# Order edges on VectorE, spread loads and two more half buffers in a Strassen matmul chain on one Trainium2 core

## The chip, the cores and the metric

One core of a Trainium2 chip runs the whole program. TensorE (PE) multiplies, ScalarE (ACT) and VectorE (DVE) work on elements, SyncE (SP) issues every DMA of the part that changes, GpSimd (POOL) has almost nothing to do. Each engine takes its instructions in the order written for it and waits at an instruction whose inputs or whose output buffer are not ready. The metric is the device time of the program in microseconds (us), lower is better.

## The reference

```python
# q, k, v: 8 x 8 heads x 576 x 64
q_s = np.exp(q - np.max(q, axis=-1, keepdims=True))
q_s = q_s / (np.sum(q_s, axis=-1, keepdims=True) + 1e-09)
...                                            # k_s the same, along axis 2
kv = np.einsum('bhsd,bhse->bhde', k_s, v)
attn_out = np.einsum('bhsd,bhde->bhse', q_s, kv)
x = np.ascontiguousarray(attn_out.transpose(0, 2, 1, 3)).reshape(B * S, H * D)   # 4608 x 512
...
h = x @ w_in                                   # first pair of weights, 512 -> 2048 -> 512
g = h * (1.0 / (1.0 + np.exp(-1.702 * h)))
x = g @ w_out
...
h = x @ w_in                                   # second pair of weights, the same sizes
g = np.where(h >= 1, h, np.where(h <= -1, 0.0, (h + 1) ** 2 / 4))
out = g @ w_out
```

The weights arrive in float64 and are converted on the chip.

## The kernel before

The scheduler of the language decides the order on each engine: the program is written in one order, and rows of an engine may be moved past each other by the scheduler's own estimate of when inputs are there. An order edge (`add_manual_dep` with `NoSync`) fixes that one row stands behind another on the same engine; it adds no semaphore.

**Stages.** (1) Attention and the first matrix `x @ w1_in` run block by block: 9 blocks (`NB`) of 512 tokens, 16 steps (`NM`) each (`gemm1`, `act`, lines 720 to 742); results `g0` go to DRAM, one store per two steps from one of three buffers `sg`. (2) `out_pass(0, ...)` computes `g @ w1_out`. (3) `pass_in` computes `x1 @ w2_in` and the activation, stores `g1`, and in its first part also converts `w2_out` ("the last weight's conversion"). (4) `out_pass(1, ...)` computes `g1 @ w2_out`.

**Strassen form.** Stages 2 to 4 multiply 2 x 2 block matrices with seven products instead of eight, in the order `PROD = (1, 7, 6, 2, 5, 4, 3)`. A matrix product in float32 is done as three matmuls, with each operand split into a high and a low part: `hi` is a rounded copy (ACT, line 104), `lo = src - hi` (DVE, line 105). The operands of products 7, 6 and 5 are sums of two quadrants and need a DVE instruction before the split (`operand`, through `tt`, line 108, "SUM" below); products 1, 2, 4 and 3 take a quadrant as it stands. Product 2 is followed by `last_sum`, which makes the operand of product 4.

**An out pass.** 5 column groups `j` (`HALVES`: 512, 512, 512, 384, 384 columns), 7 products, 4 pieces `i` of the inner dimension: 140 steps, 28 per group. In a group, steps 0 to 3 are product 1, 4 to 7 product 7, 8 to 11 product 6, 12 to 15 product 2, 16 to 19 product 5, then 4 and 3. A step is 12 matmuls (`gemm`), and behind `gemm(s)` stands `ready(s + 3)`, which makes the operand pair three steps ahead. The pairs live in 7 slots (`R_AT` = 16, 17, 18, 19, 24, 25, 26) taken in turn: `hi` of step s takes the slot that `lo` of step s - 4 had, `lo` of step s that of `hi` of step s - 3. So `hi(s)` can start once gemm(s - 4) is through, and `lo(s)` once gemm(s - 3) is.

**Slots.** 27 tiles of 128 x 1024 float32, named `s0` to `s26`: 0 to 15 hold the four quadrants (`G_AT`), in `pass_in` 4 to 15 and 20, 21 its operand pairs (`C_AT`), 22 to 26 its results on their way to DRAM (`E_AT`), 16 to 19 the weight conversion (`W_AT`: raw data, halves, sums, and `hls`, the output buffers of 256 elements x 2). Seven weight buffers `w` of 2 MB serve all passes in turn.

**Between the passes.** The first steps of an out pass are prepared in the last steps of the stage ahead (`ready0`, `ready1`), and its quadrants and weights are loaded there. Slots 24 to 26 are not free yet at that time: ahead of pass 0 slots 20 to 26 do not exist until the first stage's buffers are released, ahead of pass 1 slots 22 to 26 hold results that are being stored. A DMA that SP issues waits for the DMA issued eight before it.

Of the kernel before, what the change touches and what calls it, by code (L numbers as in the profile page):

```python
# [8 lines left out]
FP32 = mybir.dt.float32  # L9
FP32R = mybir.dt.float32r  # L10
# [3 lines left out]
ALU = mybir.AluOpType  # L14
# [4 lines left out]
def kernel(  # L19
# [11 lines left out]
    nc = tc.nc  # L31
# [8 lines left out]
    NM = DFF // P  # L40
# [61 lines left out]

    def split(hi, lo, src):
        nc.scalar.activation(out=hi, in_=src, func=ACTF.Copy)  # L104
        nc.vector.tensor_tensor(out=lo, in0=src, in1=hi.bitcast(FP32), op=ALU.subtract)  # L105

    def tt(o, x, y, op):
        nc.vector.tensor_tensor(out=o, in0=x, in1=y, op=op)  # L108


    def weight_sets(width, raws, f12, f_r, f_s, hls):
# [70 lines left out]
    def load_weight(sl, w, p):  # L182
        sl[p] = wslot()
        nc.sync.dma_start(out=sl[p].bitcast(FP32), in_=wp_dram[w, p])
# [5 lines left out]

    def operand(bq, p, i):
        b11, b12, b21, b22 = (bq[qd][i] if qd in bq else None for qd in ("11", "12", "21", "22"))
        if p == 7:
            tt(b12, b22, b12, ALU.subtract)
        elif p == 6:
            tt(b11, b12, b11, ALU.add)
        elif p == 5:
            tt(b12, b22, b11, ALU.subtract)
        return {1: b11, 7: b12, 6: b11, 2: b21, 5: b12, 4: b21, 3: b22}[p]


    def last_sum(bq, i):
# [25 lines left out]
    def slot(i, dt=FP32):  # L228
        return rooms["s", i].tile([P, 2, TB], dt, tag=f"s{i}", name=f"s{i}")
# [35 lines left out]
    class Tokens:  # L265
# [9 lines left out]

        def ready(self, j, p):
            n = HALVES[j]
            src = operand(self.t[j], p, 0)
            hi, lo = (slot(C_AT[p] + i, FP32R)[:, :, :n] for i in range(2))
            split(hi, lo, src)  # L280
            self.ops[j, p] = hi, lo
            if p == 2:
                last_sum(self.t[j], 0)


    def out_pass(ph, gq, sl):
        ops = {}
        zs = {}

        steps = [(j, p, i) for j in range(NJ) for p in PROD for i in range(4)]  # L290

        def ready(s):
            if s >= len(steps):
                return
            j, p, i = steps[s]
            src = operand(gq.t[j], p, i)
            n = HALVES[j]
            hi, lo = (slot(R_AT[(2 * s + x) % len(R_AT)], FP32R)[:, :, :n] for x in range(2))
            split(hi, lo, src)
            ops[s] = hi, lo  # L300
            if p == 2:
                last_sum(gq.t[j], i)

        def gemm(s):
            j, p, i = steps[s]
            n = HALVES[j]
            if p in OPENS and i == 0:
                zs[Z_OF[p]] = bank(OPENS.index(p))
            z = zs[Z_OF[p]]
            hi, lo = ops.pop(s)  # L310
            w = sl[p]
            for m in range(2):
                for c in range(2):
                    o = slice(c * 256 + m * P, c * 256 + (m + 1) * P)
                    wh, wl = w[:, 0, i, o], w[:, 1, i, o]
                    trio = ((wh, hi), (wh, lo), (wl, hi))
                    for x, (a, b) in enumerate(trio):
                        nc.tensor.matmul(  # L318
                            out=z[:, m, :n], lhsT=a, rhs=b[:, c, :],
                            start=(p in OPENS and i == 0 and c == 0 and x == 0),  # L320
                            stop=(i == 3 and c == 1 and x == 2),
                            skip_group_check=True,
                        )

        late = []

        def store(j, a, b, t):
            n, t0 = HALVES[j], STARTS[j]
            if not ph:
                nc.sync.dma_start(out=x1_dram[j, a, b], in_=t)  # L330
            else:
                late.append((j, a, b, t))

        def turn():
            for j, a, b, t in late:
                n, t0 = HALVES[j], STARTS[j]
                n4 = n // 4
                pt = bank(2, "pt").rearrange("p a c -> p (a c)").rearrange("p (r d) -> p r d", r=4)
                for r in range(4):
                    for m in range(2):  # L340
                        nc.tensor.transpose(  # L341
                            out=pt[:n4, r, m * P:(m + 1) * P], in_=t[:, m, r * n4:(r + 1) * n4], identity=ident
                        )
                u = slot(23).rearrange("p a c -> p (a c)").rearrange("p (r d) -> p r d", r=4)
                nc.scalar.activation(out=u[:n4], in_=pt[:n4], func=ACTF.Copy)
                r0 = t0 + b * n
                nc.sync.dma_start(
                    out=out[r0:r0 + n, a * 256:(a + 1) * 256].rearrange("(r p) d -> p r d", r=4),
                    in_=u[:n4],
                )  # L350
            late.clear()

        tmp = {}

        def post(j, p):
            n = HALVES[j]
            z = zs[Z_OF[p]][:, :, :n]

            def new(name):
                at = O_AT[name] if name in O_AT else (20 if ph else 23)  # L360
                return slot(at)[:, :, :n]

            def keep(name):
                t = new(name)
                nc.scalar.activation(out=t, in_=z, func=ACTF.Copy)
                return t

            if p == 1:
                zs["x"] = bank(3, "zx")
                nc.scalar.activation(out=zs["x"][:, :, :n], in_=z, func=ACTF.Copy)  # L370
            elif p == 7:
                tmp["s7"] = keep("s7")
            elif p == 6:
                tmp["u2"] = keep("u2")
            elif p == 2:
                store(j, 0, 0, keep("c11"))
            elif p == 5:
                tt(tmp["s7"], tmp["s7"], z, ALU.add)
                store(j, 1, 1, tmp["s7"])
            elif p == 4:  # L380
                tt(tmp["u2"], tmp["u2"], z, ALU.add)
                store(j, 1, 0, tmp["u2"])
            else:
                store(j, 0, 1, keep("c12"))

        LA = 3

        def run(hooks, done):
            for s in range(done, LA):
                ready(s)  # L390
            for s, (j, p, i) in enumerate(steps):
                gemm(s)
                if i == 2 and ph:
                    turn()
                if i == 3:
                    post(j, p)
                    if j + 1 < NJ:
                        for qd in {2: ("11",), 5: ("12",), 4: ("22", "21")}.get(p, ()):
                            gq.load(j + 1, qd)
                    else:  # L400
                        for f, a in hooks.get(p, ()):
                            f(*a)
                ready(s + LA)
            if ph:
                turn()

        return ready, run


    def pass_in(xq, sl, hooks):  # L410
        wr = [slot(i).rearrange("p a c -> p (a c)") for i in W_AT]
        load_set, convert_set, sum_set = weight_sets(
            128, [wr[0]], [wr[1][:, :512], wr[1][:, 512:]], wr[2][:, :512], wr[2][:, 512:768],
            [wr[3][:, :512], wr[3][:, 512:]],
        )
        n_new = [0]
        zs = {}
# [93 lines left out]
    with ExitStack() as st0:  # L511
# [234 lines left out]
        def at(s, f, *a):  # L746
            todo.append((s, len(todo), f, a))
# [39 lines left out]
                at(s0 + 4 + part + 0.5, sum_set, w, si, part)  # L787
        for p in PROD[:3]:
            at(NM + 8 * 12 + 1, load_weight, w_out1, "out1", p)
        for i, p in enumerate(PROD[3:]):  # L790
            at((NB - 1) * NM + 4 * i + 3, load_weight, w_out1, "out1", p)
        for i in range(2):
            at(NB * NM - 3 + i, ready0, i)
        todo.sort(key=lambda t: t[:2])
        jobs = {}
        for key, _, f, a in todo:
# [38 lines left out]
        for s in range(NB * NM):  # L835
            if s == (NB - 1) * NM:
                st1.close()
                open_room("s0", "left", range(NH), [P, 2, TB])
                open_room("p1", "left", (2, 3), [P, 2, TB])
                for qd in ("11", "12", "22", "21"):  # L840
                    g0.load(0, qd)
            gemm1(s)
            if s % 2 == 1:
                act(s)
            for f, a in jobs.get(s, ()):
                f(*a)
        widen(3, w_out1[1])
        widen(2, w_out1[1])
    open_room("s1", "right", range(NH, 27), [P, 2, TB])

    hooks = {p: [(load_weight, (w_in2, "in2", p))] for p in PROD}
    hooks[2].insert(0, (xq.load, (0,)))
# [5 lines left out]
    def lw(p):  # L858
        return load_weight, (w_out2, "out2", p)
# [3 lines left out]
        7: [lw(7), (g1.load, (0, "12", (2, 3)))],  # L863
        6: [(g1.load, (0, "22", (0, 1))), (ready1, (0,))],
        2: [(g1.load, (0, "22", (2, 3))), lw(6), (ready1, (1,))],
        5: [(g1.load, (0, "21", (0, 1)))],
        4: [(g1.load, (0, "21", (2, 3))), lw(2)],
        3: [lw(5), lw(4), lw(3)],
    }
    pass_in(xq, w_in2, hooks)  # L870
    run1({}, 2)


# [28 lines left out]
```

## Time and profile before

| what | value |
|---|---|
| median of 3 runs | 1627.42 us (1627.15 to 1629.46) |
| the profiled execution | 1628.26 us, span from first to last instruction 1626.5 us |
| PE busy | 1573.0 us (97%) |
| DVE, ACT busy | 1154.4 us (71%), 946.9 us (58%) |
| mean granted TensorE clock | 0.992 |
| DMA over the span | 202 GB/s |

PE is the engine to look at: what it doesn't work, and where it works at a lower clock, is what a change of order can win. A busy share near 100% in a stage says that nothing else decides there.

### The profile page before, as it was taken

What the parts mean: (1) busy time and instruction counts of PE and PEld (TensorE: products, weight loads), DVE (VectorE), ACT (ScalarE), POOL (GpSimd) and SP (SyncE); (2) the same over time, 40 slices, a digit from 0 to 9 for tenths busy, and PEclk for the clock granted to TensorE, in tenths of its full rate; (3) what the DMA queues carried; (4) which work ended last, traced back from release to release, by engine and by line L of the source; (5) the groups of instructions that cost most, each with busy time, mean ns of one, the idle gap of its engine ahead of it and who ended that gap; (6) DMA issues with size and microseconds to landing.
All of it is one profiled execution on the core that took longest, in us unless ns stands there. A gap on an engine that the chain in (4) does not pass through costs nothing. (4 is left out here: it accounts for less than half of the span.)

```text
span 1626.5 us, 20715 instructions
## 1 busy us (share of the span) xinstructions
PE 1573.0 (97%) x7588; PEld 1345.8 (83%) x7588; DVE 1154.4 (71%) x1519; ACT 946.9 (58%) x1135; POOL 8.1 (0%) x45
## 2 busy tenths in 40 slices
PE   5899999999999999999999999999998999999998
PEld 3678888888877788888999877788997788888998
DVE  7999788788744558686777787876454766766673
ACT  4867776786842344443445787877775444454453
POOL 0000000000000000000000000000000000000000
PEclk9999999999999999999999999999999999999999
DMA  8778788788759461715369767664247852524421
GB/s 217 223 235 269 264 266 258 271 271 271 270 199 369 161 202 59 230 47 175 107 205 331 284 230 261 224 236 164 107 169 312 350 178 90 170 76 131 135 73 39
DMA packets 218869, 330.61 MB, mean 203 GB/s; under 512 B 90128, under 2 KB 162832, under 8 KB 216080
## 3 DMA queue, kind: packets, MB, share of 16 engines
q1 hardware_dynamic: 218768, 329.30, 59.8%
q8 instruction: 59, 0.97, 0.2%
q14 instruction: 42, 0.34, 0.1%
HBM read 190.84 MB, written 138.41 MB: 202 GB/s over the span
## 5 line engine op out<-in xcount | busy, mean ns | idle before, releaser
L104 ACT ACTIVATE s<-s 128x1024 fp32r<-128x1024 f32 (+2 forms) x363 | 325.8, 901 | 404.2 <-PE z L318 204.3
L105 DVE TENSOR_TENSOR s<-s,s 128x1024 fp32r<-128x1024 f32 (+2 forms) x363 | 369.9, 1025 | 199.6 <-PE z L318 84.0
L318 PE MATMUL z<-s,w 128*128 128x512 f32 (+1 forms) x1920 | 409.5, 372 | 14.3 <-ACT s L104 8.1
L318 PEld LDWEIGHTS z<-s,w 128*128 128x128 f32 x1920 | 352.7, 190 | 63.4 <-ACT s L104 9.0
L318 PE MATMUL zx<-s,w 128*128 128x512 f32 (+1 forms) x1440 | 303.2, 368 | 0.0
L318 PEld LDWEIGHTS zx<-s,w 128*128 128x128 f32 x1440 | 261.7, 188 | 33.3
L732 PE MATMUL hps<-xh,w 128*128 128x512 f32 x576 | 238.2, 414 | 6.5 <-ACT w L104 4.7
L734 PE MATMUL hps<-xh,w 128*128 128x512 f32 x576 | 227.2, 394 | 1.1 <-DVE w L105 1.1
L733 PE MATMUL hps<-xl,w 128*128 128x512 f32 x576 | 226.5, 393 | 0.0
L108 DVE TENSOR_TENSOR s<-s,s 128x1024 f32<-128x1024 f32 (+2 forms) x196 | 205.6, 1060 | 28.8 <-DMA s<-g 21.8
L432 PE MATMUL z<-s,w 128*128 128x512 f32 (+1 forms) x960 | 206.9, 367 | 0.0
L432 PEld LDWEIGHTS z<-s,w 128*128 128x128 f32 x960 | 175.0, 188 | 22.5
L432 PE MATMUL zx<-s,w 128*128 128x512 f32 (+1 forms) x720 | 159.2, 369 | 5.4 <-ACT zx L464 4.0
L432 PEld LDWEIGHTS zx<-s,w 128*128 128x128 f32 x720 | 130.4, 188 | 26.6 <-ACT zx L464 7.3
L732 PEld LDWEIGHTS hps<-xh,w 128*128 128x128 f32 x576 | 109.1, 189 | 33.4 <-ACT w L104 5.6
L741 DVE TENSOR_TENSOR sg<-hps,sg 128x1024 f32<-128x1024 f32 x72 | 87.7, 1219 | 63.8 <-ACT sg L740 63.6
L734 PEld LDWEIGHTS hps<-xh,w 128*128 128x128 f32 x576 | 108.7, 189 | 25.9 <-DVE w L105 2.2
L733 PEld LDWEIGHTS hps<-xl,w 128*128 128x128 f32 x576 | 108.9, 189 | 21.3 <-issue 1.1
L740 ACT ACTIVATE sg<-hps 128x1024 f32<-128x1024 f32 x72 | 73.8, 1026 | 86.1 <-PE hps L734 71.6
L451 ACT ACTIVATE s<-s 128x1024 f32<-128x1024 f32 (+1 forms) x80 | 77.3, 969 | 1.3
L452 DVE SCALAR_TENSOR_TENSOR s<-z,s 128x1024 f32<-128x1024 f32 (+1 forms) x20 | 22.3, 1117 | 54.4 <-ACT s L451 54.2
L452 DVE SCALAR_TENSOR_TENSOR s<-s,s 128x1024 f32<-128x1024 f32 (+1 forms) x40 | 44.7, 1117 | 13.5 <-ACT s L451 12.5
(76 smaller groups left out, 1262.8 us busy)
## 6 DMA issues: line engine op xcount, KB each, us to landing
s<-g SPq DMA_DIRECT2D x96, 512.0 KB, 4.3
g<-sg SPq DMA_DIRECT2D x72, 512.0 KB, 3.2
w<-wp_out SPq DMA_DIRECT2D x14, 2048.0 KB, 12.6
g<-s SPq DMA_DIRECT2D x48, 512.0 KB, 3.0
s<-g SPq DMA_DIRECT2D x48, 384.0 KB, 3.7
wp_out<-w SPq DMA_DIRECT2D x28, 512.0 KB, 4.2
wp_in<-w SPq DMA_DIRECT2D x28, 512.0 KB, 3.9
w<-wp_in SPq DMA_DIRECT2D x7, 2048.0 KB, 8.5
```

The costliest lines, as they stand in the source:

```text
L104: nc.scalar.activation(out=hi, in_=src, func=ACTF.Copy)
L105: nc.vector.tensor_tensor(out=lo, in0=src, in1=hi.bitcast(FP32), op=ALU.subtract)
L108: nc.vector.tensor_tensor(out=o, in0=x, in1=y, op=op)
L318: nc.tensor.matmul(out=z[:, m, :n], lhsT=a, rhs=b[:, c, :], start=(p in OPENS and i == 0 and c == 0 and x == 0), stop=(i == 3 and c == 1 a ...
L432: nc.tensor.matmul(out=z[:, m, :n], lhsT=a, rhs=b[:, c, :], start=(p in OPENS and c == 0 and x == 0), stop=(c == 1 and x == 2), skip_group ...
L451: nc.scalar.activation(out=t, in_=t, func=ACTF.Square)
L452: nc.vector.scalar_tensor_tensor(out=t, in0=h, scalar=1.0, in1=t, op0=ALU.max, op1=ALU.min)
L732: nc.tensor.matmul(out=hps, lhsT=wh, rhs=xh[:, kk, :], start=(kk == 0), stop=False)
L733: nc.tensor.matmul(out=hps, lhsT=wh, rhs=xl[:, kk, :], start=False, stop=False)
L734: nc.tensor.matmul(out=hps, lhsT=wl, rhs=xh[:, kk, :], start=False, stop=(kk == KD - 1))
L740: nc.scalar.activation(out=sg, in_=hps, func=ACTF.Sigmoid, scale=1.702)
L741: nc.vector.tensor_tensor(out=sg, in0=hps, in1=sg, op=ALU.mult)
```

## The change

Three things. First, `behind` puts an order edge from the low part of each step of an out pass to the SUM of the next step, so that DVE does LO of step s ahead of the SUM of step s + 1. Second, loads between passes are moved: before pass 0 the quadrants come at four places of the last block instead of all at its start, and four weights later; before pass 1 three steps instead of two are prepared early, the third in slots 12 and 13, and quadrant "21" comes later. Third, `hls` of the last weight's conversion has four half buffers; the two new ones lie in the raw buffer.

```diff
     def split(hi, lo, src):
         nc.scalar.activation(out=hi, in_=src, func=ACTF.Copy)
-        nc.vector.tensor_tensor(out=lo, in0=src, in1=hi.bitcast(FP32), op=ALU.subtract)
+        return nc.vector.tensor_tensor(out=lo, in0=src, in1=hi.bitcast(FP32), op=ALU.subtract)
+
+    def behind(ins, other):
+        if ins is not None and other is not None:
+            tc.add_manual_dep(
+                getattr(ins, "ins", ins),
+                getattr(other, "ins", other).name,
+                mybir.DependencyInfo(mybir.DependencyClass.NoSync, mybir.DependencyReason.DATA),
+                reason="order of need",
+            )
...
-            src = operand(gq.t[j], p, i)
+            src, ins = operand(gq.t[j], p, i)
+            behind(ins, last.get("lo"))
             n = HALVES[j]
-            hi, lo = (slot(R_AT[(2 * s + x) % len(R_AT)], FP32R)[:, :, :n] for x in range(2))
-            split(hi, lo, src)
+            if ph and s == 2:
+                at = (12, 13)
+            else:
+                k = 2 * (s - 1 if ph and s > 2 else s)
+                at = [R_AT[(k + x) % len(R_AT)] for x in range(2)]
+            hi, lo = (slot(x, FP32R)[:, :, :n] for x in at)
+            last["lo"] = split(hi, lo, src)
...
-            [wr[3][:, :512], wr[3][:, 512:]],
+            [wr[3][:, :512], wr[3][:, 512:], wr[0][:, :512], wr[0][:, 512:]],
...
-        for i, p in enumerate(PROD[3:]):
-            at((NB - 1) * NM + 4 * i + 3, load_weight, w_out1, "out1", p)
+        s0 = (NB - 1) * NM
+        at(s0 + 4, g0.load, 0, "12")
+        at(s0 + 8, g0.load, 0, "22")
+        at(s0 + 15, load_weight, w_out1, "out1", 2)
+        at(s0 + 15, g0.load, 0, "21")
         for i in range(2):
-            at(NB * NM - 3 + i, ready0, i)
+            at(s0 + 13 + i, ready0, i)
...
-                for qd in ("11", "12", "22", "21"):
-                    g0.load(0, qd)
+                g0.load(0, "11")
...
+    for p in PROD[4:]:
+        load_weight(w_out1, "out1", p)
...
-        5: [(g1.load, (0, "21", (0, 1)))],
-        4: [(g1.load, (0, "21", (2, 3))), lw(2)],
-        3: [lw(5), lw(4), lw(3)],
+        5: [(ready1, (2,))],
+        4: [],
+        3: [lw(2), (g1.load, (0, "21", (2, 3, 0, 1))), lw(5), lw(4), lw(3)],
     }
     pass_in(xq, w_in2, hooks)
-    run1({}, 2)
+    run1({}, 3)
```

Three places show what the edges and the moves do to the order. The first is DVE in pass 0, second column group, from product 1 into products 7 and 6. Line 105 is LO (105 in both), line 108 (118 after) is SUM; `s4_5109` to `s7_5115` become the operands of steps 4 to 7, `s0_5033` to `s3_5039` those of 8 to 11. Before:

```order
L108 TENSOR_TENSOR s6_5113<-s10_5187,s6_5113 128x1024
L108 TENSOR_TENSOR s0_5033<-s4_5109,s0_5033 128x1024
L105 TENSOR_TENSOR s19_5248<-s1_5035,s18_5247 128x1024
L108 TENSOR_TENSOR s7_5115<-s11_5189,s7_5115 128x1024
L105 TENSOR_TENSOR s25_5267<-s2_5037,s24_5266 128x1024
L108 TENSOR_TENSOR s1_5035<-s5_5111,s1_5035 128x1024
L108 TENSOR_TENSOR s2_5037<-s6_5113,s2_5037 128x1024
L105 TENSOR_TENSOR s16_5284<-s3_5039,s26_5283 128x1024
L108 TENSOR_TENSOR s3_5039<-s7_5115,s3_5039 128x1024
L105 TENSOR_TENSOR s18_5301<-s4_5109,s17_5300 128x1024
```

and after:

```order
L105 TENSOR_TENSOR s19_5248<-s1_5035,s18_5247 128x1024
L105 TENSOR_TENSOR s25_5267<-s2_5037,s24_5266 128x1024
L105 TENSOR_TENSOR s16_5284<-s3_5039,s26_5283 128x1024
L118 TENSOR_TENSOR s4_5109<-s8_5183,s4_5109 128x1024
L105 TENSOR_TENSOR s18_5301<-s4_5109,s17_5300 128x1024
L118 TENSOR_TENSOR s5_5111<-s9_5185,s5_5111 128x1024
L105 TENSOR_TENSOR s24_5318<-s5_5111,s19_5317 128x1024
L118 TENSOR_TENSOR s6_5113<-s10_5187,s6_5113 128x1024
L105 TENSOR_TENSOR s26_5337<-s6_5113,s25_5336 128x1024
L118 TENSOR_TENSOR s7_5115<-s11_5189,s7_5115 128x1024
```

The SUMs of steps 4 to 11, which were done before the LO of step 4, now alternate with the LOs, step by step.

The second place is DVE at the start of pass 1. The first row of each piece is the last result of `pass_in`; `s2_9739` and `s3_9741` are the operands of steps 2 and 3, `s4_9987` and `s5_9989` those of steps 4 and 5. Before:

```order
L452 SCALAR_TENSOR_TENSOR s22_10119<-zx_9983,s22_10119 128x2x384
L108 TENSOR_TENSOR s4_9987<-s8_10026,s4_9987 128x1024
L108 TENSOR_TENSOR s0_9735<-s4_9987,s0_9735 128x1024
L105 TENSOR_TENSOR s18_10165<-s4_9987,s17_10164 128x1024
L108 TENSOR_TENSOR s5_9989<-s9_10028,s5_9989 128x1024
L108 TENSOR_TENSOR s6_10008<-s10_10051,s6_10008 128x1024
L108 TENSOR_TENSOR s1_9737<-s5_9989,s1_9737 128x1024
L108 TENSOR_TENSOR s7_10010<-s11_10053,s7_10010 128x1024
L108 TENSOR_TENSOR s4_9987<-s8_10026,s0_9735 128x1024
L105 TENSOR_TENSOR s25_10131<-s2_9739,s24_10130 128x1024
```

and after, where the LO of step 2 (into slot 13) stands earlier, among the results of `pass_in`:

```order
L470 SCALAR_TENSOR_TENSOR s22_10113<-zx_9983,s22_10113 128x2x384
L105 TENSOR_TENSOR s25_10148<-s3_9741,s24_10147 128x1024
L118 TENSOR_TENSOR s4_9987<-s8_10026,s4_9987 128x1024
L105 TENSOR_TENSOR s16_10165<-s4_9987,s26_10164 128x1024
L118 TENSOR_TENSOR s5_9989<-s9_10028,s5_9989 128x1024
L105 TENSOR_TENSOR s18_10182<-s5_9989,s17_10181 128x1024
L118 TENSOR_TENSOR s6_10008<-s10_10051,s6_10008 128x1024
L105 TENSOR_TENSOR s24_10201<-s6_10008,s19_10200 128x1024
```

The LO that writes slot 25 belonged to step 2 and stood behind seven SUMs; now one of step 3 writes it, and every SUM stands behind it.

The third place is SP at the same point of the program: `w` are weights of `w2_out`, `g1_4...` the last results of `pass_in`, `s8` to `s15` quadrants of pass 1. Before:

```order
L253 DMA s11_10053<-g1_0113_197 128x1024
L184 DMA w_10055<-wp_out2_6_85 128x4096
L455 DMA g1_4113_261<-s25_10074 256x1x384
L253 DMA s12_10079<-g1_0100_190 128x1024
L253 DMA s13_10081<-g1_0101_191 128x1024
L455 DMA g1_4103_257<-s26_10096 256x1x384
L253 DMA s14_10101<-g1_0102_192 128x1024
```

and after:

```order
L264 DMA s11_10053<-g1_0113_197 128x1024
L194 DMA w_10055<-wp_out2_6_85 128x4096
L473 DMA g1_4113_261<-s25_10074 256x1x384
L473 DMA g1_4103_257<-s26_10096 256x1x384
L473 DMA g1_4013_253<-s22_10113 256x1x384
L194 DMA w_10118<-wp_out2_2_86 128x4096
L264 DMA s14_10120<-g1_0102_192 128x1024
```

What stands ahead of the store from slot 25 is the same as before, the 2 MB weight right ahead of it included; the loads of quadrant "21" that stood behind it moved back.

## Rows read from the trace of the kernel before

**Rows 1.** Windows by stage: busy us of each engine, then clock, DMA share, GB/s.

```profile
40.00:80.00 40.00, 33.48 (x160) 25.65 (x158) 39.00 (x82) 34.62 (x48) 0.80 (x4) 1.00 0.73 215
536.00:566.00 30.00, 26.43 (x102) 20.69 (x101) 18.43 (x16) 12.24 (x13) 0.00 (x0) 0.89 0.31 120
566.00:900.00 334.00, 334.00 (x1633) 296.58 (x1632) 235.83 (x219) 154.35 (x164) 0.00 (x0) 1.00 0.51 171
900.00:1242.00 342.00, 336.60 (x1630) 294.98 (x1629) 235.58 (x300) 254.65 (x316) 0.00 (x0) 1.00 0.58 208
1242.10:1279.00 36.90, 26.12 (x99) 19.82 (x98) 25.62 (x23) 13.24 (x15) 0.00 (x0) 0.86 1.02 424
1279.00:1617.00 338.00, 338.00 (x1726) 301.37 (x1724) 226.12 (x208) 162.43 (x170) 0.00 (x0) 1.00 0.39 124
```

**Rows 2.** Groups by line, PE: busy, mean ns, then idle before and what ended it.

```profile
L318 PE MATMUL z<-s,w 128*128 128x512 f32 (+1 forms) x1920 | 409.5, 372 | 14.3 <-ACT s L104 8.1 <-DVE s L105 6.2
L432 PE MATMUL zx<-s,w 128*128 128x512 f32 (+1 forms) x720 | 159.2, 369 | 5.4 <-ACT zx L464 4.0 <-DVE s L108 1.2
```

**Rows 3.** PE in runs: timeline of pass 0, then chain that ended last (384 columns).

```profile
565.05 11.04 PE L318 MATMUL zx<-s,w 128*128 128x512 f32 x48
575.93 11.04 PE L318 MATMUL z<-s,w 128*128 128x512 f32 x48
...
1575.00 8.32 PE zx L318 x48
```

**Rows 4.** Timeline of ACT and DVE in the steady part of pass 0.

```profile
660.22 1.06 ACT L104 ACTIVATE s<-s 128x1024 fp32r<-128x1024 f32 x1 [1.66 <-PE z L318]
660.52 1.22 DVE L105 TENSOR_TENSOR s<-s,s 128x1024 fp32r<-128x1024 f32 x1 [1.49 <-PE z L318]
```

**Rows 5.** Timeline from `pass_in` into pass 1, all engines.

```profile
1242.12 5.64 PE L318 MATMUL z<-s,w 128*128 128x512 f32 x24
1248.11 0.32 SPq L184 DMA_DIRECT2D w<-wp_out  x1
1249.40 0.52 SPq L455 DMA_DIRECT2D g<-s  x1
1251.82 2.48 DVE L108 TENSOR_TENSOR s<-s,s 128x1024 f32<-128x1024 f32 x2 [5.91 <-DMA s<-g]
1253.14 2.02 ACT L104 ACTIVATE s<-s 128x1024 fp32r<-128x1024 f32 x2 [8.22 <-DVE s L108]
1254.23 1.23 DVE L105 TENSOR_TENSOR s<-s,s 128x1024 fp32r<-128x1024 f32 x1
1255.38 5.76 DVE L108 TENSOR_TENSOR s<-s,s 128x1024 f32<-128x1024 f32 x5
1262.52 1.22 DVE L105 TENSOR_TENSOR s<-s,s 128x1024 fp32r<-128x1024 f32 x1 [1.38 <-DMA g<-s]
1263.80 15.27 PE L318 MATMUL z<-s,w 128*128 128x512 f32 x58 [3.82 <-DVE s L105]
1278.90 11.04 PE L318 MATMUL zx<-s,w 128*128 128x512 f32 x48
```

**Rows 6.** Timeline from the last block into pass 0, all engines.

```profile
519.52 0.50 PE L732 MATMUL hps<-xh,w 128*128 128x512 f32 x1 [1.27 <-DVE sg L741]
535.98 5.83 PE L318 MATMUL z<-s,w 128*128 128x512 f32 x25
545.57 2.95 ACT L104 ACTIVATE s<-s 128x1024 fp32r<-128x1024 f32 x3 [3.12 <-PE z L318]
547.63 0.49 PE L318 MATMUL z<-s,w 128*128 128x512 f32 x1 [1.64 <-ACT s L104]
```

**Rows 7.** Timeline in `pass_in`, 384 columns (768 elements): DVE SUM, ACT behind it.

```profile
1224.20 0.94 DVE L108 TENSOR_TENSOR s<-s,zx 128x768 f32<-128x768 f32 x1
1225.18 0.94 ACT L450 ACTIVATE s<-s,half 128x768 f32<-128x768 f32 x1 [1.89 <-DVE s L108]
```

**Rows 8.** Waits of ACT in `pass_in`: us in total, times, longest.

```profile
ACT s L104 <- DMA wp_out<-s: 16.8, 18, 1.8
```

More of the change, by code (lines that the diff above doesn't have):

```diff
@@ L104, in split @@
         nc.scalar.activation(out=hi, in_=src, func=ACTF.Copy)
-        nc.vector.tensor_tensor(out=lo, in0=src, in1=hi.bitcast(FP32), op=ALU.subtract)
+        return nc.vector.tensor_tensor(out=lo, in0=src, in1=hi.bitcast(FP32), op=ALU.subtract)
[7 more added lines that the diff above has]
+            )
     def tt(o, x, y, op):
-        nc.vector.tensor_tensor(out=o, in0=x, in1=y, op=op)
+        return nc.vector.tensor_tensor(out=o, in0=x, in1=y, op=op)
     def weight_sets(width, raws, f12, f_r, f_s, hls):
@@ L192, in operand @@
         b11, b12, b21, b22 = (bq[qd][i] if qd in bq else None for qd in ("11", "12", "21", "22"))
+        ins = None
         if p == 7:
-            tt(b12, b22, b12, ALU.subtract)
+            ins = tt(b12, b22, b12, ALU.subtract)
         elif p == 6:
-            tt(b11, b12, b11, ALU.add)
+            ins = tt(b11, b12, b11, ALU.add)
         elif p == 5:
-            tt(b12, b22, b11, ALU.subtract)
-        return {1: b11, 7: b12, 6: b11, 2: b21, 5: b12, 4: b21, 3: b22}[p]
+            ins = tt(b12, b22, b11, ALU.subtract)
+        return {1: b11, 7: b12, 6: b11, 2: b21, 5: b12, 4: b21, 3: b22}[p], ins
     def last_sum(bq, i):
@@ L277, in ready @@
             n = HALVES[j]
-            src = operand(self.t[j], p, 0)
+            src, _ = operand(self.t[j], p, 0)
             hi, lo = (slot(C_AT[p] + i, FP32R)[:, :, :n] for i in range(2))
@@ L288, in out_pass @@
         zs = {}
+        last = {}
         steps = [(j, p, i) for j in range(NJ) for p in PROD for i in range(4)]
```

## Prediction

> **What bounds the kernel now.** I read the windows by stage first. In them a stage in which PE is busy all the time can only get slower, and a stage with a gap can win at most the gap and the clock lost behind it. Pass 0 after its start and pass 1 after its start have no gap at all: 334.0 of 334 us and 338.0 of 338 us busy, clock 1.00. Stages with gaps are the start of pass 0 (26.43 of 30 us, clock 0.89), `pass_in` (336.60 of 342) and the start of pass 1 (26.12 of 36.9, clock 0.86) [rows 1]. The groups by line say who ends PE's waits: in the two out passes 14.3 us in front of line 318, all of it behind a hi or a LO, in `pass_in` 5.4 us, most behind the copy of z to zx [rows 2]. So the whole prize is some 20 us of gaps and about 6 us of low clock, and the 672 us of full work are at stake.
>
> **PE's own pace.** 48 matmuls of 512 columns follow each other in 575.93 - 565.05 = 10.88 us, 0.2267 each, a step of 12 in 2.72 us; with 384 columns 8.32 / 48 = 0.1733, a step in 2.08 us [rows 3]. In the steady part ACT and DVE wait for PE to give back a slot [rows 4], so hi and LO run as early as the seven slots let them.
>
> **The edges in the steady part.** Before, the SUMs of products 7 and 6 were done ahead of the LO of step 4. After, DVE must do SUM(s), then wait for ACT's hi(s), then LO(s), then SUM(s+1). That loop is seen once in the trace: SUM at 1251.82, hi behind it at 1253.14 (1.32), LO at 1254.23 (1.09), the next DVE row at 1255.38 (1.15) [rows 5]. Sum 3.56 us a step against 2.72 of PE: each step with a SUM loses 0.84.
> How much is in hand? Count from the start of a group. LO(3) starts when gemm(0) ends, at 2.72. SUM(4) 3.87, LO(4) 6.28, and PE can use a LO 1.28 after its start (1262.52 to 1263.80 [rows 5]): 7.56. The second matmul of step 4 wants it at 4 x 2.72 + 0.23 = 11.11. In hand 3.55. There are seven more steps: 3.55 - 7 x 0.84 = -2.33 at step 11. PE's order after has five matmuls of step 12 pulled in between those of steps 10 and 11, which fill 1.13. Left: 1.2 us of gap.
> Product 5 has its own loop of four: LO(15) starts when gemm(12) ends, two last sums stand behind it (1.15 + 2 x 1.14 = 3.43), hi(16) 4.75, LO(16) 5.84, usable 7.12, wanted at 3 x 2.72 + 0.23 = 8.39. In hand 1.27, less 3 x 0.84: 1.25 late. So 2.4 us for a group of 512.
> With 384 columns SUM to ACT is 0.98 [rows 7]; the other two links I scale by elements to about 0.87 and 0.90: 2.75 against 2.08, 0.67 a step. In hand 2.67 and 0.9, late 2.0 and 1.1, less 0.87 pulled in: 2.2 us.
> Pass 0: two groups x 2.4, two x 2.2, and 1.2 for product 5 of the first: **+10.4**. Pass 1 has the same edges, but the transposes of `turn` stand in PE's queue, eight in each of four steps of a group, and give the loop time. Bounds 0 and 10.4; I take **+4.0**, nearer to nothing, since they lengthen PE's own pace just where the loop runs.
>
> **Start of pass 1.** Three steps are prepared now, 36 x 0.2267 = 8.16 us of work from 1242.12, so PE runs to 1250.3 instead of 1247.6. Step 3 then needs slots 24 and 25. The store that frees 25 was issued at 1249.40, right behind a 2 MB weight (1248.11), and LO into 25 went at 1262.52, with a DMA as the releaser [rows 5]. 13 us at the stage's 424 GB/s [rows 1] is 5.5 MB: the store landed behind all that had been issued ahead of it. SP's order up to this store is unchanged, so it lands at the same time; moving "21" back takes away only what stood behind. LO(3) goes at 1262.5 again, and PE goes on at 1263.8 again, with 37 matmuls done. Before had 38: products 1 and 7 have 96, and 58 were left [rows 5]. So the third step wins nothing by then. Behind LO(3) on DVE is every SUM. Before, seven SUMs were done by then, and step 11 ended at 1278.90 + 10.88 = 1289.8. After: LO(4) at 1262.5 + 3.56 = 1266.1, usable 1267.4, step 11's 7 x 3.56 later, 1292.3, its end 1294.8, less the 1.1 pulled in: **+3.9**. Both wait long enough for a lower clock; after, its cost lies under the loop's waits.
>
> **Start of pass 0.** Before: 1.27 us wait for the product of `sg` [rows 6], which stood on DVE behind SUMs that had been drawn forward; then 96 matmuls from 535.98 to 565.05 [rows 3, 6], 29.1 us for 21.8 at pace, 7.3 lost to gaps and the clock behind them. hi(2) and hi(3) stood on ACT behind hi of steps 4, 5 and 8, the last of which waited for a slot of gemm(4) (545.57), and PE for them until 547.63 [rows 6]. Together 8.6. After, no SUM stands ahead of the last `sg`, and hi(2), hi(3) come first. But nothing is done ahead: hi(3) goes into slot 26, which I take to lie on the last `sg` buffer, whose store goes out only after the last product of the block. I take LO(3) 7.4 after PE's start, between 3.9 (as in the steady part) and later than hi(2) came before (11.7), LO(4) usable 1.1 late, then 7 x 0.84, less 1.1: 5.9 lost. Net **-2.7** (bounds: -7.4 with slot 26 free at once, -1.3 with only the first wait won). The loads come 2 MB at a time; weights 5, 4 and 3, issued last, are wanted 16 steps (43 us) later, which hides them.
>
> **The conversion.** ACT waits 16.8 us for half buffers to be stored [rows 8], and some of that reaches PE as part of the 5.4 us. Two more buffers take most of ACT's wait, but they are the raw buffer, whose next load must now wait for them, and SP has results queued behind that load. Between +3 and -5.4; I take half of PE's wait, **-2.7**.
>
> **The sum.** 10.4 + 4.0 + 3.9 - 2.7 - 2.7 = +12.9 us on the profiled execution of 1628.26 (span 1626.5 and 1.8 around it), which lies 0.84 above the median of 1627.42. On the median: **1640.3**, slower by 0.8%. A difference under 0.2% (3.3 us) can't be told from no change here.
>
> **The rivals.**
> *The loop is absorbed (faster).* Place: steps 4 to 11 of each group. It decides where the loop is under 2.72 + 3.55/7 = 3.2 us: then PE never waits in the steady part. Steady 0, start of pass 0 about -6.5, of pass 1 about 0, conversion -2.7: 1618. For it: ACT and DVE have idle time in the passes, and the loop of 3.56 is one reading in a busy stretch. Against: its three links are fixed delays from start to start, with nobody queued between. Chance 0.13.
> *The store of slot 25 lands early.* If it need not wait for what was issued ahead, LO(3) goes at 1254, step 11 ends 4.7 us earlier than before instead of 3.9 later: +4.3, 1631.7. Against: 13 us from issue to landing. Chance 0.10.
> *Half and half (no change).* Losses in the steady part half as large (+7.2), the conversion gives all its 5.4 and pass 0 its 7 us: 3.9 + 7.2 - 12.4, about 1626 to 1629. Chance 0.13.
> *The clock falls in the late steps.* Gaps of 0.8 us in each 3.56 could cost TensorE its clock; a step at the lower level of 1.2 GHz takes 5.4 us, 1.9 more than the loop. Without gaps the clock would come back, so about one such step in each of 18 loops: +34 on top, 1674. Against: from 40 to 80 us PE was busy 33.48 of 40 us in many pieces, and 1.00 was granted [rows 1]; the low clock is seen in windows with gaps of several us. Chance 0.04. (The Trainium skill, TensorE: Matmul & The Clock Gate, section on psum-queue depth-cycling, tells of a kernel whose short idle pieces between groups of matmuls made the clock go to and fro; by that rule this rival would be the likeliest. The window at 40 to 80 us doesn't agree.)
>
> **Numbers.** My forecast has 0.60. The range 1624 to 1650 leaves out the absorbed loop (0.13) and the clock (0.04); its upper end takes pass 1 at its bound of 10.4 and the conversion at +3. The absorbed loop and a little of the even case are faster, most of the even case is the same: 0.16, 0.12, and 0.72 slower.
>
> **What would show it.** Right: PE's idle in the middle of pass 0 goes from 0 to about 10 us, in pieces under 1 us in front of a LO, near the ends of products 6 and 5; DVE alternates SUM and LO there, with 1.2 us idle before LO, ended by ACT. At the start of pass 1 one gap of some 13 us from 1250 to 1264, ended by a LO that waits for a store. No wait for `sg`, and clock 1.00 at the start of pass 0. Fewer waits of ACT for `wp_out`. Wrong: PE 100% busy through both passes; or a gap under 5 us at the start of pass 1.

## The result: slower by 1.1%, and the profile after

The changed kernel takes 1644.87 us (median of 4 runs, 1644.37 to 1647.8) against 1627.77 of the kernel before: ratio 1.0107, 95% interval 1.009 to 1.0125, +17.1 us. The profiled execution's span is 1642.6 us, 16.1 more. The forecast was 1640.3, inside 1624 to 1650, slower.

First the windows of the kernel after, one for each stage: first 12 steps of pass 0, rest of pass 0, `pass_in`, first 12 steps of pass 1, rest (columns: window, length, busy us of PE, PEld, DVE, ACT, POOL, then clock, DMA share, GB/s). They answer to [rows 1].

```profile
535.29:570.56 35.27, 34.52 (x151) 27.73 (x149) 26.39 (x23) 15.96 (x17) 0.00 (x0) 1.00 0.52 204
570.56:895.19 324.63, 318.46 (x1537) 277.46 (x1536) 228.62 (x216) 145.25 (x153) 0.00 (x0) 1.00 0.48 163
895.19:1247.44 352.25, 348.07 (x1676) 303.64 (x1676) 237.97 (x304) 261.73 (x322) 0.00 (x0) 1.00 0.60 213
1247.44:1300.40 52.96, 37.84 (x150) 28.58 (x150) 26.31 (x24) 17.61 (x19) 0.00 (x0) 0.87 0.87 364
1300.40:1637.40 337.00, 334.11 (x1692) 293.57 (x1690) 219.16 (x207) 158.04 (x167) 0.00 (x0) 1.00 0.36 115
```

Before, the same five stages took 39.95, 312.35, 353.84, 47.66 and 331.51 us, from the starts of PE's runs (535.98, 575.93, 888.28, 1242.12, 1289.78, end of the last run 1621.29). After, five matmuls of step 12 are run before product 6 ends, in either pass (5 x 0.2267 = 1.13 us), and five of `pass_in` before pass 0 ends. With that moved back, the stages changed by -6.5 (with 0.7 from the earlier start), +12.3, -0.5, +4.2 and +6.6: in all 16.1. Both passes, full before, now have PE idle.

Who ends PE's waits (us in total, times, longest), against [rows 2]:

```profile
PE z L336 <- DVE s L105: 9.1, 4, 7.8
...
PE zx L336 <- DVE s L105: 8.3, 26, 0.5
...
PE z L336 <- ACT s L104: 6.2, 3, 4.7
```

The middle row is new: 26 short waits in front of zx (products 6 and 5), every one for a LO. The timeline of such a place, the middle of a group of 512 in pass 0 (of the rows between, those that bear on the turn):

```profile
634.89 1.23 DVE L105 TENSOR_TENSOR s<-s,s 128x1024 fp32r<-128x1024 f32 x1 [1.19 <-ACT s L104]
636.04 1.22 DVE L118 TENSOR_TENSOR s<-s,s 128x1024 f32<-128x1024 f32 x1
637.29 1.06 ACT L104 ACTIVATE s<-s 128x1024 fp32r<-128x1024 f32 x1
638.38 1.22 DVE L105 TENSOR_TENSOR s<-s,s 128x1024 fp32r<-128x1024 f32 x1 [1.13 <-ACT s L104]
639.53 1.22 DVE L118 TENSOR_TENSOR s<-s,s 128x1024 f32<-128x1024 f32 x1
639.66 3.06 PE L336 MATMUL zx<-s,w 128*128 128x512 f32 x12 [0.44 <-DVE s L105]
640.78 1.06 ACT L104 ACTIVATE s<-s 128x1024 fp32r<-128x1024 f32 x1 [0.86 <-DVE s L118]
641.87 1.22 DVE L105 TENSOR_TENSOR s<-s,s 128x1024 fp32r<-128x1024 f32 x1 [1.12 <-ACT s L104]
643.15 3.04 PE L336 MATMUL zx<-s,w 128*128 128x512 f32 x12 [0.20 <-DVE s L105]
```

LO, SUM, hi, LO: from LO to LO (634.89, 638.38, 641.87) one turn takes 3.49 us, with DVE idle 1.1 to 1.2 us in each before its LO. PE's step follows at the same 3.49 (639.66 to 643.15), where its own pace is 2.72.

The start of pass 1, against [rows 5] (again without the rows that don't bear on it):

```profile
1247.44 8.36 PE L336 MATMUL z<-s,w 128*128 128x512 f32 x36
1254.72 3.03 SPq L473 DMA_DIRECT2D g<-s  x3
1259.44 1.06 ACT L104 ACTIVATE s<-s 128x1024 fp32r<-128x1024 f32 x1 [9.08 <-DMA g<-s]
1260.55 0.79 PE L336 MATMUL z<-s,w 128*128 128x512 f32 x1 [4.75 <-ACT s L104]
1267.86 1.22 DVE L105 TENSOR_TENSOR s<-s,s 128x1024 fp32r<-128x1024 f32 x1 [16.37 <-DMA g<-s]
1269.14 7.16 PE L336 MATMUL z<-s,w 128*128 128x512 f32 x24 [7.80 <-DVE s L105]
1276.66 3.01 PE L336 MATMUL z<-s,w 128*128 128x512 f32 x12 [0.35 <-DVE s L105]
1280.15 3.01 PE L336 MATMUL z<-s,w 128*128 128x512 f32 x12 [0.47 <-DVE s L105]
```

Three prepared steps (x36), then one matmul when the hi of step 3 is there (1260.55), then nothing until the LO of step 3, which DVE starts when the store out of slot 25 has landed. From the start of the pass to PE's first matmul behind that LO are 1269.14 - 1247.44 = 21.70 us; before, to the first matmul behind the LO into the same slot, 1263.80 - 1242.12 = 21.68. Then steps of 3.49 us.

### The profile page after: what moved, and what is told of

It reads as the page before. It is cut to its first block, busy times and chain, and to the rows that moved or that the text cites. A ratio compares the mean times of both kernels' runs of the same rounds, so it can differ in the third digit from the quotient of the medians.

```text
span 1642.6 us, 20595 instructions
## 1 busy us (share of the span) xinstructions
PE 1581.5 (96%) x7588; PEld 1340.7 (82%) x7588; DVE 1144.4 (70%) x1519; ACT 947.6 (58%) x1135; POOL 8.1 (0%) x45
## 5 line engine op out<-in xcount | busy, mean ns | idle before, releaser
L336 PE MATMUL zx<-s,w 128*128 128x512 f32 (+1 forms) x1440 | 318.3, 372 | 8.7 <-DVE s L105 8.3
L450 PE MATMUL zx<-s,w 128*128 128x512 f32 (+1 forms) x720 | 159.5, 370 | 4.1 <-ACT zx L482 2.6
L468 ACT ACTIVATE s<-s,half 128x1024 f32<-128x1024 f32 (+1 forms) x40 | 42.5, 1062 | 25.7 <-DVE s L118 25.5
## 6 DMA issues: line engine op xcount, KB each, us to landing
w<-wp_out SPq DMA_DIRECT2D x14, 2048.0 KB, 13.1
```

What stands on the lines that cost most here:

```text
L336: nc.tensor.matmul(out=z[:, m, :n], lhsT=a, rhs=b[:, c, :], start=(p in OPENS and i == 0 and c == 0 and x == 0), stop=(i == 3 and c == 1 a ...
L450: nc.tensor.matmul(out=z[:, m, :n], lhsT=a, rhs=b[:, c, :], start=(p in OPENS and c == 0 and x == 0), stop=(c == 1 and x == 2), skip_group ...
L468: nc.scalar.activation(out=t, in_=h, func=ACTF.Relu, scale=0.5, bias=half)
```

## The experiments

The table has, of every kernel's profiled execution, the start of pass 0 and the five stages, from the starts of PE's runs. "rest" is the pass behind its 12th step. Ratios are to runs of the kernel before in the same session; its medians there were 1626.46 (edges_only, no_edges, two_back, four_bufs), 1626.89 (two_back_two_bufs, weight6_late, own_queue, queue_two_bufs), 1627.32 (edges_p5, late_two_bufs, start_slots) and 1626.6 us (edges_p76). Kernels marked * have five matmuls of later work in the first 12 steps (ten in edges_p76).

| kernel | median us | ratio to before, 95% interval | pass 0 starts | 12 steps | rest | pass_in | 12 steps | rest |
|---|---|---|---|---|---|---|---|---|
| before | 1627.8 | | 535.98 | 39.95 | 312.35 | 353.84 | 47.66 | 331.51 |
| after * | 1644.9 | 1.0107 (1.009, 1.0125) | 535.29 | 35.27 | 324.63 | 352.25 | 52.96 | 337.00 |
| edges_only * | 1649.6 | 1.0149 (1.0133, 1.0164) | 535.77 | 35.80 | 324.63 | 351.03 | 57.30 | 337.07 |
| no_edges | 1630.3 | 1.002 (1.0012, 1.0029) | 536.28 | 38.70 | 312.35 | 355.60 | 48.90 | 331.50 |
| two_back | 1625.1 | 0.9991 (0.9982, 0.9999) | 536.82 | 32.64 | 312.35 | 356.63 | 47.85 | 331.51 |
| four_bufs | 1631.6 | 1.0036 (1.0023, 1.0049) | 538.36 | 38.46 | 312.34 | 356.26 | 47.67 | 331.50 |
| edges_p5 | 1626.5 | 0.9992 (0.9983, 1.0001) | 538.45 | 37.06 | 312.42 | 351.48 | 48.67 | 331.51 |
| edges_p76 * | 1643.4 | 1.0107 (1.0092, 1.0122) | 535.94 | 36.98 | 317.95 | 353.12 | 57.98 | 333.48 |
| two_back_two_bufs | 1618.1 | 0.9952 (0.994, 0.9964) | 537.02 | 32.64 | 312.65 | 352.41 | 47.97 | 331.50 |
| weight6_late | 1620.9 | 0.9962 (0.995, 0.9974) | 536.08 | 32.64 | 312.90 | 357.13 | 43.39 | 331.50 |
| own_queue | 1620.2 | 0.9967 (0.9955, 0.998) | 534.72 | 32.64 | 312.62 | 356.77 | 45.03 | 331.50 |
| queue_two_bufs | 1617.8 | 0.9946 (0.9933, 0.9958) | 534.59 | 32.64 | 312.34 | 353.14 | 45.32 | 331.51 |
| late_two_bufs | 1615.1 | 0.9928 (0.9916, 0.9941) | 534.47 | 32.64 | 312.35 | 352.08 | 42.66 | 331.50 |
| start_slots | 1609.6 | 0.9892 (0.9878, 0.9905) | 536.95 | 32.64 | 312.76 | 351.38 | 36.69 | 331.51 |

(The expectations cut the stages by a count of matmuls; their figures for a stage lie up to 1.6 us from the table's, the same in all kernels of a kind.)

**The edges alone, and the rest without them.** edges_only is the kernel before with `behind` and its call; no_edges is the kernel after without the call:

```diff
-            behind(ins, last.get("lo"))
```

> The kernel before with the order edges alone; loads, slots, prepared steps and half buffers as before. Theory of the loop (SUM, then hi, then LO, then the next SUM takes 3.56 us where PE needs 2.72): steady part of pass 0 about +10, steady part of pass 1 about +5, start of pass 1 about +4, start of pass 0 -1 to -3 since no SUM stands ahead of the last sg product any more: 1641 to 1648 us. Rival, the moved loads and slots make the loss and the edges are absorbed by the slack of the slots: within 3 us of 1627.

> The changed kernel without the order edges; loads, slots, three prepared steps and four half buffers stay. Theory of the loop: the 10 us of pass 0 and the 5 us of pass 1 come back, the gain at the start of pass 0 (-6.5 in the trace after) stays in part, the conversion gives 1 to 3: 1616 to 1626 us, faster than both. Rival (loads and slots make the loss): 1638 us or more, near the changed kernel.

Measured: +23 us for the edges alone, a little above the expectation and more than the whole change. Their rest of pass 0 and of pass 1 is that of the kernel after to 0.1 us, and without the edges both are those of before to 0.01. So the edges make the loss of the steady parts, all of it, and the moved loads and slots none. They also make most of the gain at the start of pass 0: 35.80 with them alone, 38.70 with the moved loads alone. With the edges, the third prepared step and the loads moved with it are together worth 4.3 us at the start of pass 1 (57.30 against 52.96). no_edges, at 1630.3, fell between its expectation and its rival: it keeps little of pass 0's gain, and its `pass_in` got longer.

**Edges two steps back.** SUM(s) stands behind LO(s-2):

```diff
-            behind(ins, last.get("lo"))
+            behind(ins, last.get("lo1"))
...
-            last["lo"] = split(hi, lo, src)
+            last["lo1"] = last.get("lo")
+            last["lo"] = split(hi, lo, src)
```

> The changed kernel, but SUM(s) is placed behind LO(s-2) and no longer behind LO(s-1), so that a SUM runs while ACT makes the hi of the step before. Theory of the loop: one turn of 3.56 us now covers two steps, less than PE's 2.72 each, so the steady part of both passes loses nothing and the start of pass 1 no longer pays 3.56 a step: 1616 to 1626 us, faster than both. Rival 1 (any such edge hurts because SUMs have to be done early): 1638 us or more. Rival 2 (loads and slots make the loss): 1638 us or more.

Measured: 1625.12, as expected, 19.8 us below the kernel after (18.4, if each is taken against the kernel before of its own session: +17.1 and -1.3). One window shows it, the rest of pass 0:

```profile
569.46:881.81 312.35, 312.35 (x1537) 278.64 (x1536) 230.67 (x217) 145.67 (x154) 0.00 (x0) 1.00 0.48 170
```

PE is busy 312.35 of 312.35 us. The same SUMs still stand behind LOs, only one step further back, and cost nothing: it is the serial turn through ACT that costs, not that SUMs may no longer run ahead. The first 12 steps of pass 0 take 32.64 = 144 x 0.2267, PE's full pace.

**One product's edges.** The call stands behind `if p == 5:` in edges_p5 and `if p in (7, 6):` in edges_p76, both on the kernel before.

> The kernel before with the order edges for product 5 alone. Theory of the loop: product 5 has a loop of its own, worth 1.25 us in a group of 512 and 1.1 in one of 384, 5.95 in pass 0, and about half of that in pass 1 as in the changed kernel; the starts of the passes as before: +8 to +10, 1635 to 1637 us. In pass 0 after its first 12 steps 318 to 319 us (312.5 before, 326.2 with all edges). Rival (the loss of a group is one loss, paid once wherever SUMs are held back): as much as with all edges, 326. Rival (product 5 is absorbed, products 7 and 6 make it all): within 3 us of 1627.

> The kernel before with the order edges for products 7 and 6 alone, the counterpart of edges_p5. Theory of the loop: in the changed kernel a group of 512 lost 1.39 us by the end of product 6 and 1.32 in product 5; with the edges of product 5 gone the second part goes, and pass 0 after its first 12 steps takes 318 to 320 us (312.5 before, 326.2 with all edges); start of pass 1 about +8 and start of pass 0 about -5.5 as with all edges; in all +9 to +14, 1636 to 1641. Rival (product 5 is without effect, products 7 and 6 make the whole loss, as edges_p5 alone could be read): 326 us in that stretch and 1648 or more.

Measured: product 5's edges alone cost nothing (a miss), those of 7 and 6 alone 320.2 in the rest of pass 0 with the ten early matmuls (317.95 + 2.27), +7.9 of the 12.3, at the upper end of what was expected there; in all 1643.4, 2.4 us above the expected range. The parts don't add, and DVE's rows suggest why: first after, then edges_p5.

```profile
650.03 2.46 DVE L105 TENSOR_TENSOR s<-s,s 128x1024 fp32r<-128x1024 f32 x2
652.41 3.49 DVE L118 TENSOR_TENSOR s<-s,s 128x1024 f32<-128x1024 f32 x3
657.11 1.23 DVE L105 TENSOR_TENSOR s<-s,s 128x1024 fp32r<-128x1024 f32 x1 [1.21 <-ACT s L104]
```

```profile
654.65 1.22 DVE L105 TENSOR_TENSOR s<-s,s 128x1024 fp32r<-128x1024 f32 x1 [0.24 <-PE z L332]
655.79 2.35 DVE L118 TENSOR_TENSOR s<-s,s 128x1024 f32<-128x1024 f32 x2
658.22 1.23 DVE L105 TENSOR_TENSOR s<-s,s 128x1024 fp32r<-128x1024 f32 x1
661.79 1.23 DVE L105 TENSOR_TENSOR s<-s,s 128x1024 fp32r<-128x1024 f32 x1 [1.21 <-ACT s L104]
```

After, two last sums and SUM(16) stand between LO(15), at about 651.2, and LO(16): 5.9 us. In edges_p5 the scheduler puts SUM(16) directly behind LO(15) and one last sum behind it: 658.22 - 654.65 = 3.57. The loop turns in 3.57 there too, but starts 2.3 us earlier, and by the prediction's own account (8.39 - 3.57 - 1.28 - 3 x 0.84) 1.0 us is left in hand at its end. So, by these rows, the price of the edges hangs on what the scheduler puts in front of the first SUM; no run changes that alone.

**Four half buffers.** Alone on the kernel before, and taken back on two_back:

```diff
-            [wr[3][:, :512], wr[3][:, 512:]],
+            [wr[3][:, :512], wr[3][:, 512:], wr[0][:, :512], wr[0][:, 512:]],
```

> The kernel before with four half buffers in the last weight's conversion and nothing else. From the fall of PE's waits in pass_in (5.4 to 4.1 us) I expect -1.3: 1625.5 to 1627.5 us, hardly to be told from before. My prediction's value was -2.7 (1624.7). Rival, the raw buffer is given back later and SP's queue backs up: +3 (1630).

> The kernel two_back with two half buffers in the last weight's conversion, as before, instead of four. From four_bufs, whose pass_in took 356.1 us against 353.7 of before: 2 to 4 us below two_back. Rival (the loss of four_bufs has nothing to do with the buffers): within 1 us of two_back.

Measured: `pass_in` 2.4 us longer with four on the kernel before, 4.2 on two_back; medians +5.1 and +7.0, the latter more than expected and across two sessions (of four_bufs' +5.1, 2.4 us stand before pass 0 in its profile, where nothing differs). Two more pairs of the table differ in the buffers alone: weight6_late and late_two_bufs by 5.1 us in `pass_in`, own_queue and queue_two_bufs by 3.6. So four half buffers cost time, as the rival said. Waits of ACT and DVE in `pass_in`, of before, of four_bufs and of edges_only (two half buffers), against [rows 8]:

```profile
ACT s L92 <- DMA s<-in_moe_w_out_dram: 3.2, 3, 2.1
...
DVE s L94 <- DMA s<-in_moe_w_out_dram: 2.3, 4, 1.0
```

```profile
DVE s L94 <- DMA s<-in_moe_w_out_dram: 14.4, 9, 2.2
...
ACT s L92 <- DMA s<-in_moe_w_out_dram: 10.0, 9, 2.4
...
ACT s L104 <- DMA wp_out<-s: 3.4, 6, 1.2
```

```profile
DVE s L94 <- DMA s<-in_moe_w_out_dram: 14.1, 8, 3.3
...
ACT s L92 <- DMA s<-in_moe_w_out_dram: 7.2, 6, 2.2
```

ACT's wait for half buffers does fall, from 16.8 to 3.4. But the raw buffer is now lent out, its next load is late, and the conversion waits for it at the head of both engines' queues: 14.4 on DVE and 10.0 on ACT, where the trace of before has 2.3 and 3.2. The copy of z to zx, for which PE waits, is queued behind. That the late loads make the loss is argued from these waits and not shown, and one trace speaks against it: edges_only waits 14.1 and 7.2 us for the same loads, with two half buffers, and its `pass_in` is the shortest of the table (351.03). No run has four buffers and a raw buffer of its own, so the cause of the loss stays open.

**The start of pass 1.** Three edits on two_back: weight 6 behind the last result stores; these stores on a queue of their own; both with two half buffers in queue_two_bufs and late_two_bufs.

```diff
-        2: [(g1.load, (0, "22", (2, 3))), lw(6), (ready1, (1,))],
+        2: [(g1.load, (0, "22", (2, 3))), (ready1, (1,))],
...
-        3: [lw(2), (g1.load, (0, "21", (2, 3, 0, 1))), lw(5), lw(4), lw(3)],
+        3: [lw(6), lw(2), (g1.load, (0, "21", (2, 3, 0, 1))), lw(5), lw(4), lw(3)],
```

```diff
-                nc.sync.dma_start(out=g1_dram[j, a, b, g], in_=t)
+                queue = nc.gpsimd if (j, g) == (NJ - 1, 3) else nc.sync
+                queue.dma_start(out=g1_dram[j, a, b, g], in_=t)
```

> The kernel two_back with the load of weight 6 of the second output pass moved behind the last four result stores (from the hook of product 2 to that of product 3). Theory (step 3 of pass 1 waits because the store that frees slot 25 is issued behind weight 6 on SP and lands behind all that is in flight): the store goes out at about 1239 instead of 1245.6, LO(3) follows about 5 us earlier, first 12 steps of pass 1 in 42 to 44 us instead of 47.6; in all 4 to 6 us below two_back. Rival (the load of the quadrants for product 7 sets the time anyway, or weight 6 is then late for step 8): within 1.5 us of two_back.

> The kernel two_back with the last four result stores of pass_in issued by the idle GpSimd on a queue of its own. Theory (those stores land late because of what was issued ahead of them on SP's queue): hi(3) and LO(3) no longer wait for 18 us but for a few, the next wait is SUM(4) behind its load at 1248 (10 us after the start of the pass), first 12 steps of pass 1 in 36 to 40 us instead of 47.6; 8 to 11 us below two_back. Rival (the DMA engines are full with what SP has issued, so that the stores land as late from any queue): within 2 us of two_back.

> Both of the last two edits on two_back: the last four result stores on GpSimd's queue, and two half buffers. If each theory holds, the gains add: 10 to 15 us below two_back, 1610 to 1615 us, the fastest here. If one of them falls, only the other's share.

> Edges two steps back, two half buffers, and weight 6 behind the last result stores. The gains of two_back_two_bufs (pass_in 352.3) and of weight6_late (first 12 steps of pass 1 in 42.7 us) in one kernel: 1612 to 1615 us. Rival (they share a cause): 1617 to 1618.

Measured: weight6_late takes 4.5 us off the first 12 steps (47.85 to 43.39), as expected, and late_two_bufs reaches 1615.07, the upper end of what was expected. own_queue took the first 12 steps to 45.03, not to 36 to 40, a gain of 2.8 us, and its median is 4.9 below that of two_back, not 8 to 11:

```profile
1243.49 1.06 ACT L104 ACTIVATE s<-s 128x1024 fp32r<-128x1024 f32 x1 [6.17 <-DMA g<-s]
...
1245.32 0.96 DVE L471 SCALAR_TENSOR_TENSOR s<-s,s 128x768 f32<-128x768 f32 x1 [8.11 <-ACT s L470]
...
1246.57 0.69 POOL L475 DMA_DIRECT2D g<-s  x1 [8.37 <-DVE s L471]
...
1256.01 2.00 ACT L104 ACTIVATE s<-s 128x1024 fp32r<-128x1024 f32 x2 [3.21 <-DMA g<-s]
```

The hi of step 3 waited for its slot at the head of ACT's queue; behind it stood the last two results of `pass_in`, so their stores went out at 1246.57 and 1248.69, and the hi of step 4, which needs the first of these, at 1256.01. The wait moved from step 3 to step 4. queue_two_bufs (45.32 in the first 12 steps, 1617.8 in all) missed its 1610 to 1615 for the same reason.

**Slots that wait for no store.** start_slots is late_two_bufs with step 3 prepared with the hook of product 4 in slots 14 and 15, the "21" pieces loaded in order behind it, and

```diff
-            if ph and s == 2:
-                at = (12, 13)
-            else:
-                k = 2 * (s - 1 if ph and s > 2 else s)
+            if ph and s < 8:
+                at = ((16, 17), (18, 19), (12, 13), (14, 15), (16, 17), (18, 19), (24, 25), (26, 16))[s]
+            else:
+                k = 2 * (s - 4 if ph else s)
```

> late_two_bufs with slots for the first eight steps of pass 1 that wait for no result store up to step 5: step 3 in 14 and 15 (free since product 4 of pass_in), steps 4 and 5 in the slots of steps 0 and 1, the slots freed by the last stores only from step 6. Theory (the wait for the store of slot 25 is all that holds step 3): PE goes on through step 3; the next wait is SUM(4) behind its load, 9.6 us after the start of the pass, usable at 13.3 where PE wants it at 11.1. First 12 steps 36 to 39 us instead of 42.7: 1607 to 1611 us, the fastest. Rival (the transfers as a whole are late, so the loads of the quadrants take the place of the stores): within 1.5 us of late_two_bufs.

Measured: 36.69 us, 1609.62, the fastest here, 1.1% below the kernel before.

```profile
1233.73 11.08 PE L337 MATMUL z<-s,w 128*128 128x512 f32 x48
1243.31 1.22 DVE L118 TENSOR_TENSOR s<-s,s 128x1024 f32<-128x1024 f32 x1 [4.96 <-DMA s<-g]
1246.87 0.50 PE L337 MATMUL z<-s,w 128*128 128x512 f32 x1 [2.06 <-ACT s L104]
1248.75 10.95 PE L337 MATMUL z<-s,w 128*128 128x512 f32 x47 [1.38 <-DVE s L105]
```

PE runs through four steps (x48); the next wait is the one named, SUM(4) for its load at 9.6 us after the start.

## Why the prediction was right, and where not

| term | predicted | measured |
|---|---|---|
| steady part of pass 0 | +10.4 | +12.3 |
| steady part of pass 1 | +4.0 | +6.6 |
| start of pass 1 | +3.9 | +4.2 |
| start of pass 0 | -2.7 | -6.5 |
| conversion | -2.7 | -0.5 |
| sum | +12.9 | +16.1 |

**The loop, right.** Predicted turn 3.56, measured 3.49 in the steady part; with 384 columns 2.75 and 791.07 - 788.32 = 2.75. By PE's starts a group of 512 lost 693.12 - 614.26 - 336 x 0.2267 = 2.7 us for 2.4 predicted, 1.4 by the end of product 6 and 1.3 in product 5 (1.2 and 1.25). A group of 384 lost 833.28 - 771.95 - 336 x 0.1733 = 3.1 for 2.2: the scaled slack of products 7 and 6 was 0.7 too large there. Of this, some 0.5 can be read off: LO(3) started 774.31 - 771.95 = 2.36 us after the group's first matmul instead of 2.08, and the first two turns took 2.87 (774.31, 777.18, 780.05). In pass 1 the transposes gave less back than taken: 6.6, inside the bounds of 0 and 10.4, between which the 4.0 was a guess. The rival that the loop is absorbed is out by edges_only and two_back; half and half too, with 12.3 + 6.6 lost in the steady parts for its 7.2.

**The start of pass 1, right** step by step: the third step wins nothing against the kernel before (21.70 for 21.68 us to the LO into slot 25), then the loop, +4.2. The one gap of some 13 us came as 4.75 and 7.80, with one matmul between. That the store of slot 25 is what LO(3) waits for is shown by weight6_late and start_slots. The rival that it lands early is out: 13.1 us from issue to the LO, as before.

**The start of pass 0, too small a gain.** The failing step: "hi(3) goes into slot 26, which I take to lie on the last `sg` buffer". From the kernel after:

```profile
535.29 21.92 PE L336 MATMUL z<-s,w 128*128 128x512 f32 x96
535.51 2.00 ACT L104 ACTIVATE s<-s 128x1024 fp32r<-128x1024 f32 x2
...
536.90 0.32 SPq L760 DMA_DIRECT2D g<-sg  x1
...
538.28 1.23 DVE L105 TENSOR_TENSOR s<-s,s 128x1024 fp32r<-128x1024 f32 x1 [0.28 <-PE z L336]
```

hi(2) and hi(3) (x2) stand ahead of the last store of `sg`, which is issued at 536.90: hi(3) waited for no store. LO(3) ran at 538.28, 3.0 us after PE's start and behind gemm(0), not 7.4, so the term came out near its bound of -7.4.

**The conversion, the wrong end of its bounds.** I took half of PE's wait as gain. ACT's waits for half buffers did fall, from 16.8 to 4.3 us, and PE's idle in `pass_in` from 5.4 to 4.2, but the stage won 0.5 in place of 2.7. Nor do the buffers make that 0.5: where they are the one difference, they cost 2.4 to 5.1 us, and edges_only, with two, is shorter still (351.03 against 352.25). The prediction named a cost for its +3 (raw buffer, next load late); the waits for that load rose as it said, but that they make the loss is not shown. Why `pass_in` is shorter in edges_only and edges_p5 (351.03 and 351.48) than in before (353.84), though nothing in it was changed, stays open.

That the sum came so near is in part luck: 3.8 us more gained at pass 0 and 2.2 less in the conversion partly cancel; with the steady parts and the start of pass 1, 4.8 too small together, they leave the 3.2 us by which the forecast is short.

**The clock, right.** In the rest of pass 0 the granted clock was 1.00 with all the short waits in it. The Trainium skill (TensorE: Matmul & The Clock Gate, section on psum-queue depth-cycling) tells of a kernel in which frequent short idle pieces of PE made the clock go to and fro; read as a rule, it would do so here, and this trace doesn't agree.

## What to carry to other kernels

An order edge between two instructions of one engine closes a loop if the other engine stands between them: add up its turn from start to start, and compare it with the step of the bounding engine and the slack. If it loses, put the edge one step further back before dropping it: here that kept the whole gain at the start of pass 0 and cost nothing in the rest of either pass. A buffer put to a second use takes one wait away and may bring another to its owner, so measure it alone: here the two half buffers cost time. A prepared step wins nothing if the next one's slot waits for a transfer, as that of step 3 did here.

## What was not expected of the hardware

- **PE's idle time reads too small.** In pass 1's start steps begin 3.49 us apart (1276.66, 1280.15), 0.77 over pace, and the row shows 0.47 idle: matmul ends are modelled. Losses of PE have to be read from start to start.
- **The program's beginning comes in two forms.** The same instructions give, from 20 to 40 us, a granted clock of 0.91 in some profiles and 0.83 in others, and pass 0 starts 2.4 us later where all else is equal (four_bufs 538.36, before 535.98). It bears on spans of single profiles; whether it belongs to a program or to an execution stays open. First before, then four_bufs:

```profile
20.00:40.00 20.00, 15.79 (x73) 11.83 (x72) 16.84 (x44) 12.47 (x26) 0.20 (x1) 0.91 0.88 238
```

```profile
20.00:40.00 20.00, 16.02 (x62) 11.32 (x60) 14.29 (x39) 10.84 (x24) 0.20 (x1) 0.83 0.86 231
```

- **A second queue did shorten the landing.** The store out of slot 25 took 13.1 us from issue to the LO on SP's queue (after: 1254.72 to 1267.86) and at most 8.7 from GpSimd's (own_queue: issued 1237.52, LO at 1246.19):

```profile
1237.52 0.68 POOL L475 DMA_DIRECT2D g<-s  x1 [2.93 <-DVE s L471]
...
1246.19 1.22 DVE L105 TENSOR_TENSOR s<-s,s 128x1024 fp32r<-128x1024 f32 x1
```

  It doesn't come from fewer transfers in flight: by the landings in the same trace of own_queue, the load that SP issued 1.2 us ahead of the store, at 1236.28, landed at 1253.30, 17.0 us later. The Trainium skill (DMA: Bandwidth & Descriptors, section Issuing engines are not separate DMA queues) says that this saves only the time to issue; here it was more.
